# Attention and two gated layers on one core: v's loads moved from SyncE's queue to GpSimd's, q and k requested earlier into more tiles

## The chip, the cores and the metric

The kernel runs on one core of a Trainium2 chip. The time is device microseconds (us) of one execution. A core has TensorE (PE; its weight loads are shown as PEld), VectorE (DVE), ScalarE (ACT), GpSimd (POOL) and SyncE (SP), each with an instruction queue that runs in order, and 16 DMA engines that all queues share.

## The reference

```python
def _attn_ref(q, k, v):                       # each (4, 12, 448, 64)
    S = q.shape[2]
    scale = 1.0 / np.sqrt(q.shape[-1])
    scores = scale * np.matmul(q, k.transpose(0, 1, 3, 2)) - np.log(S)
    attn = 1.0 / (1.0 + np.exp(-scores))
    return np.matmul(attn, v).astype(np.float32)

def reference(**kwargs):
    attn_out = _attn_ref(**attn_kwargs)
    B, H, S, D = attn_out.shape
    x = np.ascontiguousarray(attn_out.transpose(0, 2, 1, 3)).reshape(B * S, H * D)
    x = _moe_ref(x=x, **moe_kwargs)           # x @ w_in, silu, @ w_out: 1792 x 768, 2048 wide
    return _moe2_ref(x=x, **moe2_kwargs)      # x @ w_in, a rational function, @ w_out
```

The two weight pairs of the layers come as float64 arrays, whose bits the kernel turns into float32 itself. The change touches the attention only.

## The kernel before

The program has three stages: attention, the first layer and the second layer. The first 186 us are the attention, and all that follows waits for its output.

Attention works on 24 pairs of heads (NPT). A pair i needs a k tile, a q tile and a v tile, each loaded from DRAM in pieces. `load_by_key` loads k or v of a pair in two DMAs of 128 KB and 96 KB, one for each half of the partitions. q comes in four DMAs of 56 KB, 128 bytes a piece, in a layout that VectorE's 32x32 transpose (`attn_X`) turns into the one that the matmuls need. k is put in order by a copy on GpSimd (`mix`, km from ks), transposed by TensorE (`attn_T`), and split into two parts by ScalarE and VectorE (`attn_C`).

The loop over n has 48 steps, two for each pair, and four for a group of two pairs e and e+1 (`part` is 0 to 3). TensorE's order in a step is: the score matmuls of this step (`attn_QK`, L329), the transposes of a later pair's k (L301, in every second step), and the matmuls with v for the scores of the step before (`attn_AV`, L353). In a group these are 48 score matmuls, eight transposes and 32 matmuls with v. ScalarE applies the sigmoid (L344). `attn_E` copies a finished pair out of PSUM, and for the last two of the four batches stores it in DRAM (L370).

The order on each engine is the order of the code; each queue waits for the tiles that its next instruction needs. In step n = 2i the code calls `mix(i + 2)`, then `load_qk(i + 4)`; the k tile alternates between two buffers, and so does the q tile. In part 0 it also calls `load_v(e + 2)` and `load_v(e + 3)`, into four buffers, after the last matmuls that read the pairs e-2 and e-1. All these loads are issued by SP, but for three of the first pairs' that ACT issues.

SP has other work in this stage. For the layers' weights, `conv_load` (L160) loads 768 KB of a weight into a staging tile, ScalarE and VectorE turn it into float32 (`conv`, called in the steps of `CONVS`), and `conv_out` (L176) stores 384 KB in DRAM. In step 40 (`at_half == -8`) `load_w1` (L526, tile wf) loads the first converted weights of the first layer, which `prep_ij` and `sums_12` (ACT, and DVE L398) read in step 43.

A DMA signals its landing in one of eight counters, which the queues of SP and ACT use in turn. So a load waits until the one eight before it has landed; the program shows this as a wait for DMAHW0 to DMAHW7.

Of the kernel before, what the change touches and what calls it, by code (L numbers as in the profile page):

```python
# [11 lines left out]
F32 = mybir.dt.float32  # L12
# [29 lines left out]
def attention_moe_moe(ctx: ExitStack, tc: tile.TileContext, q, k, v, w_in1, w_out1, w_in2, w_out2, a, b2, out):  # L42
    nc = tc.nc
    B, H, S, D = q.shape
    NT, DM = out.shape
    DFF = w_out1.shape[0]
    P = 128
    NCH = 4
    CP = S // NCH
    NP = H // 2  # L50
    NPT = B * NP
# [14 lines left out]
    def fixed(nm, n, shape, dt, pool=cpool):  # L66
        return [pool.tile(shape, dt, tag=f"{nm}{i}", name=f"{nm}{i}") for i in range(n)]
# [56 lines left out]
    def constants():  # L124
        nc.vector.memset(nls, NEG_LOG_S)
        nc.vector.memset(lnb[:, 0:1], ONE * 2.0**-63)
        nc.vector.memset(lnb[:, 1:2], -63.0 * math.log(2.0))
        nc.scalar.activation(absb[:, 0:1], nls, AF.Sigmoid)
        make_identity(nc, ident)
# [40 lines left out]
    def conv_outs():  # L170
        for do in outs:
            do()
        outs.clear()
# [45 lines left out]
    qs, ks, vs = {}, {}, {}  # L219
    ld_p = [None]  # L220
    ks_t = []
    LO, HI = slice(0, D), slice(D, 2 * D)
    SQ = 32

    def rest_of(i):
        return HI if i % 2 else LO

    def load_by_key(src, t, i, early=False):
        b, hp = divmod(i, NP)
        at_ = 0  # L230
        for part in (LO, HI):
            n = NCH if part == rest_of(i) else NCH - 1
            (nc.scalar if early and part == HI else nc.sync).dma_start(  # L233
                out=t[part, :, : n * D],
                in_=src[b, 2 * hp : 2 * hp + 2, at_ : at_ + n * D].rearrange("h (p c) d -> p h (c d)", c=n),
            )
            at_ += n * D

    def load_qk(i):
        if i >= NPT:  # L240
            return
        b, hp = divmod(i, NP)
        ks[i] = ks_t[i % 2]
        load_by_key(k, ks[i], i, i < 2)
        t = qs[i] = ld_p[0].tile([P, S], F32, tag="qs", name=f"qs_{i}", bufs=2)
        for part in range(2 * D // SQ):
            j, e0 = divmod(part * SQ, D)
            (nc.scalar if i == 0 and part % 2 else nc.sync).dma_start(
                out=t[part * SQ : (part + 1) * SQ, :].rearrange("l (c d) -> l c d", d=SQ),
                in_=q[b, 2 * hp + j, :, e0 : e0 + SQ].rearrange("(c l) d -> l c d", l=SQ),  # L250
            )
# [12 lines left out]
    def load_v(i):  # L264
        if i >= NPT:
            return
        vs[i] = ld_p[0].tile([P, 2, NCH * D], F32, tag="vs", name=f"vs_{i}", bufs=4)
        load_by_key(v, vs[i], i)

    xa_p, xa_s = opened("xa")  # L270
    xa_all = xa_p.tile([P, 9 * 2 * S], F32R, tag="xa_all", name="xa_all")
# [32 lines left out]
    def attn_X(i):  # L304
        x = xq[i] = ld_p[0].tile([P, S], F32, tag="xq", name=f"xq_{i}", bufs=1)
        nc.vector.transpose(x, qs.pop(i))

    def attn_C(i, p, pk, o):
        k_, q_ = st["k", i], st["q", i] = kst.get(), qst.get()
        both = ((k_, o[:, :BK]), (q_, xq.pop(i)))  # L310
        for x, src in both:
            nc.scalar.copy(x[:, 0, :], src)
        for x, src in both:
            nc.vector.tensor_tensor(out=x[:, 1, :], in0=src, in1=x[:, 0, :].bitcast(F32), op=ALU.subtract)
        if p is None:
            pairs.put(pk)
# [45 lines left out]
    def attn_E(i):  # L362
        b, hp = divmod(i, NP)
        del vs[i]
        if b < 2:
            nc.vector.tensor_copy(xk[b * KD + hp], hb[i % 2][:, :S])
            return
        t = xio.get()
        nc.vector.tensor_copy(t[:, :S], hb[i % 2][:, :S])
        nc.sync.dma_start(out=xs[0][hp][:, b * S : (b + 1) * S], in_=t[:, :S])  # L370
        xio.put(t)
# [597 lines left out]
    with tc.manual_schedule():  # L969
# [5 lines left out]
        hb.extend(hb_all[:, j] for j in range(2))  # L975
        hpair.append(hb_all)
        pairs.put(*fixed("pair", 3, [P, 2, 512], F32, ps_p))
        ks_t.extend(fixed("ks", 2, [P, 2, NCH * D], F32, ld_p[0]))
        qst.put(ld_p[0].tile([P, 2, S], F32R, tag="qx", name="qx"))
        load_qk(0)  # L980
        load_qk(1)
        for i in range(2):
            nc.vector.memset(ks_t[i][rest_of(i + 1), :, LAST * D :], 0.0)
        constants()
        warm(11)
# [2 lines left out]
        attn_C(0, *attn_T(0, hb[0]))  # L988
        warm(3)
        mix(1)  # L990
        load_qk(2)
        load_v(0)
        load_v(1)
        load_qk(3)
        conv_load()
        conv_load()

# [4 lines left out]
        for n in range(2 * NPT):  # L1002
            e, part = n // 4 * 2, n % 4
            i, h = divmod(n, 2)
            o = e + 1
            if h == 0:
                mix(i + 2)
                load_qk(i + 4)
            if n < 4:
                units = ([(e, 0), (e, 1)], [(e, 2)], [(o, 0), (o, 1)], [(o, 2), (e, LAST)])[part]  # L1010
                new = (1, 2, NPT, 3)[part]
            else:
                units = ([(e, 0), (e, 1)], [(e, 2), (o, 0)], [(o, 1), (o, 2)], [(e, LAST)])[part]
                new = i + 2 if h else NPT
            conv_outs()
            if new < NPT:
                attn_X(new)
            ready = [(u, attn_QK(*u)) for u in units]
            p = attn_T(new) if new < NPT else None
            for u, p_ in ready:  # L1020
                attn_S(*u, p_)
            for u in waiting:
                attn_AV(*u)
            waiting = units
            if part == 0:
                if e:
                    attn_E(e - 2)
                    attn_E(e - 1)
                load_v(e + 2)
                load_v(e + 3)  # L1030
            if p is not None:
                attn_C(new, *p)
            at_half = n - 2 * NPT
            if at_half >= -NOPS - 6:
                next(first_ops, None)
            flush()
            if at_half == -8:
                load_w1(0)
                load_w1(1)
            if at_half == -5:  # L1040
                xk_s.close()
                wr_p, wr_s = opened("wr")
                wr.extend(fixed("wr", 4, [P, DM], F32R, wr_p))
                wq.extend(fixed("wq", 6, [P, HM], F32R, wr_p))
                prep_ij(0)
                sums_12(0)
            if at_half == -3:
                prep_s12(0)
            if at_half == -1:
                prep_a22(0)  # L1050
            if n == 1:
                stage.put(more)
                conv_load()
                third[0] = more
            if n == 4:
                coefficients()
            if n == 12:
                coefficients_abs()
            if n in CONVS:
                conv()  # L1060
# [247 lines left out]
        for n in range(HN):  # L1308
            g, p = turn(n)
# [25 lines left out]
            if n == 3 * HF - 2:  # L1335
                gsrc.put(wif_all[:, NWS * HM : NWS * HM + BK])
                load_g2(0)
                for i in range(2):
                    t = xa_all[:, 12 * BK + i * DM : 12 * BK + (i + 1) * DM]
                    wring.put(t.rearrange("p (j e) -> p j e", j=2))  # L1340
            if n > 3 * HF:
                i = n - 3 * HF - 1
# [85 lines left out]
```

## Time and profile before

| | |
|---|---|
| median of three runs | 1072.2 us (1068.54 to 1072.66) |
| the profiled execution | 1071.1 us, its span 1069.3 us |
| TensorE busy over the span | 1040.7 us (97%) |
| VectorE, ScalarE, GpSimd busy | 772.8, 604.8, 221.1 us |
| DMA moved | 251.06 MB, mean 235 GB/s |

A busy share is an average over stages. Here the first 186 us differ from the rest: the page's line of TensorE in 40 slices reads 8989987 for them and 9 in all later slices but the last. A matmul that waits for data shows as idle time of TensorE ahead of it, with the instruction or the DMA that came last as its releaser. The issue of a DMA on SP is a row of the queue (SPq); its length is the time until the queue goes on, not the transfer.

### The profile page before, as it was taken

To read this page: it belongs to the slowest core of one execution; us is meant where nothing else is said; L and a number is where in the kernel's file an instruction comes from. 1 tells how busy PE (TensorE), PEld (TensorE's weight loads), DVE (VectorE), ACT (ScalarE), POOL (GpSimd) and SP (SyncE) were. 2 spreads that over 40 slices of the span, in tenths; PEclk is the share of its full clock that TensorE was granted. 3 is DMA by queue.
4 is the path that set the end of the run, shared out by engine and by line. 5 is a ranking of instruction groups with operands and counts; after the bars stand their busy time and mean duration, and the time that the engine had idled before them with its cause. 6 is when DMAs were issued, how large, how long until landed. Compare 5 with 4: busy or idle time off the path is not lost.

```text
span 1069.3 us, 15954 instructions
## 1 busy us (share of the span) xinstructions
PE 1040.7 (97%) x5558; PEld 895.5 (84%) x5558; DVE 772.8 (72%) x1114; ACT 604.8 (57%) x911; POOL 221.1 (21%) x173
## 2 busy tenths in 40 slices
PE   8989987999999999999999999999999999999998
PEld 4545443999998988899998888888999999999998
DVE  4648873788898757877857957779898986545761
ACT  5757874665665544432433448767777866354430
POOL 1110010000000000000000036669877942200000
PEclk9999998999999999999999999999999999999999
DMA  7978775577757676699979953666668979976651
GB/s 171 211 179 217 196 207 177 183 267 268 254 191 258 231 260 215 201 316 351 337 272 336 368 179 100 227 216 216 226 235 295 319 228 307 336 227 198 198 165 52
DMA packets 188896, 251.06 MB, mean 235 GB/s; under 512 B 57360, under 2 KB 142224, under 8 KB 188816
## 3 DMA queue, kind: packets, MB, share of 16 engines
q1 hardware_dynamic: 176736, 230.98, 66.6%
q10 hardware_dynamic: 12016, 19.06, 5.4%
q8 instruction: 43, 0.70, 0.3%
q14 instruction: 37, 0.30, 0.1%
q0 software_dynamic: 64, 0.00, 0.0%
HBM read 166.17 MB, written 83.82 MB: 234 GB/s over the span
## 4 chain that ended last, share of the span: by engine, by line
PE 69%; DVE 12%; DMA 7%; ACT 4%; SPq 3%; issue 3%; POOL 1%; ACTq 0%; DVEq 0%; POOLq 0%
PE hp L925 14%; PE acc L512 13%; PE acc L660 5%; PE acc L661 5%; PE acc L659 5%; PE hb L925 5%; PE hb L512 5%; PE hp L732 3%; PE hp L733 3%; PE hp L734 3%; DMA ks<-in_k_dram 2%; PE hb L353 2%; DVE sb L765 2%; DVE sb L763 2%; SPq L233 2%
## 5 line engine op out<-in xcount | busy, mean ns | idle before, releaser
L381 POOL TENSOR_TENSOR woL<-wif,woH 128x768 fp32r<-128x768 f32 x9 | 17.2, 1930 | 466.6 <-ACT woH L380 466.6
L344 ACT ACTIVATE sb<-pair,nls 128x896 f32<-128x896 f32 x84 | 80.4, 1006 | 30.3 <-PE pair L329 30.0
L659 PE MATMUL acc<-xa_all,woH 128*128 128x512 f32 (+1 forms) x252 | 91.9, 365 | 0.0
L661 PE MATMUL acc<-xa_all,woL 128*128 128x512 f32 (+1 forms) x252 | 91.9, 365 | 0.0
L660 PE MATMUL acc<-xa_all,woH 128*128 128x512 f32 (+1 forms) x252 | 91.9, 365 | 0.0
L353 PE MATMUL hb<-sb,vs 128*64 128x448 f32 (+1 forms) x384 | 77.0, 572 | 7.8 <-DMA vs<-in_v_dram 5.6
L761 POOL TENSOR_TENSOR sb<-sb 128x1024 f32<-128x1024 f32 (+1 forms) x32 | 70.1, 2191 | 39.4 <-ACT sb L758 39.4
L200 ACT ACTIVATE sb<-sb 128x768 f32<-128x768 f32 x64 | 58.0, 906 | 31.6 <-DMA sb<-in_moe_w_in_dram 23.4
L512 PE MATMUL acc<-xb,wr 128*128 128x448 f32 x315 | 68.1, 367 | 0.0
L512 PEld LDWEIGHTS acc<-xb,wr 128*128 128x128 f32 x315 | 59.1, 188 | 5.8 <-issue 0.7
L203 DVE SCALAR_TENSOR_TENSOR sb<-sb 128x768 int32<-128x768 int32 x64 | 61.4, 959 | 2.2
L206 DVE SCALAR_TENSOR_TENSOR sb<-sb 128x768 int32<-128x768 int32 x64 | 61.3, 958 | 2.2
L852 POOL TENSOR_TENSOR sb<-sb 128x384 f32<-128x384 f32 (+1 forms) x43 | 51.1, 1195 | 56.8 <-DMA sb<-gk 54.9
L732 PE MATMUL hp<-hx,woH 128*128 128x512 f32 (+1 forms) x168 | 61.6, 367 | 0.0
L733 PE MATMUL hp<-hx,woH 128*128 128x512 f32 (+1 forms) x168 | 61.6, 367 | 0.0
L734 PE MATMUL hp<-hx,woL 128*128 128x512 f32 (+1 forms) x168 | 61.6, 367 | 0.0
L732 PE MATMUL hp<-xa_all,woH 128*128 128x512 f32 (+1 forms) x168 | 60.7, 362 | 0.0
L734 PE MATMUL hp<-xa_all,woL 128*128 128x512 f32 (+1 forms) x168 | 60.7, 362 | 0.0
L733 PE MATMUL hp<-xa_all,woH 128*128 128x512 f32 (+1 forms) x168 | 60.7, 362 | 0.0
L763 DVE TENSOR_TENSOR sb<-hp,sb 128x768 f32<-128x768 f32 (+1 forms) x31 | 33.6, 1085 | 35.2 <-ACT sb L760 35.2
L329 PEld LDWEIGHTS pair<-xa_all 64*128 64x128 f32 x384 | 34.5, 191 | 26.3 <-issue 12.3
L353 PEld LDWEIGHTS hb<-sb,vs 128*64 128x64 f32 (+1 forms) x384 | 20.7, 138 | 38.0 <-issue 31.7
(241 smaller groups left out, 2738.4 us busy)
## 6 DMA issues: line engine op xcount, KB each, us to landing
sb<-in_moe_w_in_dram SPq DMA_DIRECT2D x32, 768.0 KB, 6.7
sb<-in_moe_w_out_dram SPq DMA_DIRECT2D x32, 768.0 KB, 6.7
gd<-sb SPq DMA_DIRECT2D x64, 224.0 KB, 3.6
wf<-w0i SPq DMA_DIRECT2D x32, 384.0 KB, 3.9
gk<-sb SPq DMA_DIRECT2D x27, 384.0 KB, 4.0
gk<-sb SPq DMA_DIRECT2D x15, 512.0 KB, 3.2
woL<-gk SPq DMA_DIRECT2D x25, 256.0 KB, 4.8
w0i<-sb SPq DMA_DIRECT2D x16, 384.0 KB, 3.2
```

The lines of the kernel that those rows point to most:

```text
L203: nc.vector.scalar_tensor_tensor(out=ui, in0=hi, scalar=SIGN_TOP, in1=ui, op0=ALU.bitwise_and, op1=ALU.bitwise_or)
L344: nc.scalar.activation(t, p[:, :, :S], AF.Sigmoid, bias=nls, scale=QKSCALE)
L353: nc.tensor.matmul(hb[i_ % 2][j * D : (j + 1) * D, :S], vs[i_][part, j, c * D : (c + 1) * D], t[part, j], start=(c == 0), stop=(c == LAST),)
L512: nc.tensor.matmul(o, w_[:, w], x[:, i_, :], start=first and kk == 0 and n_ == 0, stop=kk == HK - 1 and n_ == 2, skip_group_check=not first,)
L659: nc.tensor.matmul(o, woH[c][:, w], x[:, 0, :w_], start=(c == 0), stop=False)
L660: nc.tensor.matmul(o, woH[c][:, w], x[:, 1, :w_], start=False, stop=False)
L661: nc.tensor.matmul(o, woL[c][:, w], x[:, 0, :w_], start=False, stop=(c == KF - 1))
L732: nc.tensor.matmul(o, wh[:, w], x[:, 0, :wd_], start=first, stop=False)
L733: nc.tensor.matmul(o, wh[:, w], x[:, 1, :wd_], start=False, stop=False)
L734: nc.tensor.matmul(o, wl[:, w], x[:, 0, :wd_], start=False, stop=last)
L761: nc.gpsimd.tensor_tensor(out=q_, in0=q_, in1=a_, op=ALU.mult)
L925: nc.tensor.matmul(o, a_, y[:, w_, :], start=kk == 0 and n_ == 0, stop=kk == HF - 1 and n_ == 2)
```

## The change

Five things change. v's loads are issued by GpSimd, not by SP. k has four buffers, not two, and q three, not two (two more memsets on VectorE clear a part of the two new k tiles). The loads of k and q are calls of their own: in an even step 2i the code requests k of the pair i+5, and in the odd step after it q of the pair i+5, where before it requested both of the pair i+4 in the even step. v's loads are called in part 1 of a group instead of part 0. All loads are called after `attn_C` of the step. The order of the computing instructions on TensorE, VectorE, ScalarE and GpSimd stays as it is, but for those two memsets.

```diff
-    def load_by_key(src, t, i, early=False):
+    def load_by_key(src, t, i, eng_hi, eng=nc.sync):
...
-            (nc.scalar if early and part == HI else nc.sync).dma_start(
+            (eng_hi if part == HI else eng).dma_start(
...
-    def load_qk(i):
+    def load_k(i):
+        if i < NPT:
+            ks[i] = ks_t[i % 4]
+            load_by_key(k, ks[i], i, nc.scalar if i < 2 else nc.sync)
+
+    def load_q(i):
         if i >= NPT:
             return
         b, hp = divmod(i, NP)
-        ks[i] = ks_t[i % 2]
-        load_by_key(k, ks[i], i, i < 2)
-        t = qs[i] = ld_p[0].tile([P, S], F32, tag="qs", name=f"qs_{i}", bufs=2)
+        t = qs[i] = ld_p[0].tile([P, S], F32, tag="qs", name=f"qs_{i}", bufs=3)
...
-        load_by_key(v, vs[i], i)
+        load_by_key(v, vs[i], i, nc.gpsimd, nc.gpsimd)
...
-        ks_t.extend(fixed("ks", 2, [P, 2, NCH * D], F32, ld_p[0]))
+        ks_t.extend(fixed("ks", 4, [P, 2, NCH * D], F32, ld_p[0]))
...
-        load_qk(2)
         load_v(0)
         load_v(1)
-        load_qk(3)
+        load_k(2)
+        load_q(2)
+        load_k(3)
+        load_q(3)
+        load_k(4)
         conv_load()
         conv_load()
...
             if h == 0:
                 mix(i + 2)
-                load_qk(i + 4)
...
+            if p is not None:
+                attn_C(new, *p)
+            if h == 0:
+                load_k(i + 5)
+            if n == 0 or h:
+                load_q(i + (5 if h else 4))
+            if part == 1:
                 load_v(e + 2)
                 load_v(e + 3)
-            if p is not None:
-                attn_C(new, *p)
```

On SP, this is a piece of the queue before, from steps 6 to 10. In brackets stands what a row waits for: DMAHW is the landing of an earlier load, DVE, PE and Pool are the last readers of the buffer. ks, qs and vs are the tiles of k, q and v.

```order
L233 DMA ks_247<-in_k_dram 64x2x256 [waits DMAHW1_49,Pool_49]
L233 DMA ks_247<-in_k_dram 64x2x192 [waits DMAHW2_49]
L248 DMA qs_455<-in_q_dram 32x14x32 [waits DMAHW3_49,DVE_49]
L248 DMA qs_455<-in_q_dram 32x14x32 [waits DMAHW4_49]
L248 DMA qs_455<-in_q_dram 32x14x32 [waits DMAHW5_49]
L248 DMA qs_455<-in_q_dram 32x14x32 [waits DMAHW6_49]
L233 DMA vs_482<-in_v_dram 64x2x256 [waits DMAHW7_49,PE_49]
L233 DMA vs_482<-in_v_dram 64x2x192 [waits DMAHW0_49]
L233 DMA vs_485<-in_v_dram 64x2x192 [waits DMAHW1_49,PE_49]
L233 DMA vs_485<-in_v_dram 64x2x256 [waits DMAHW2_49]
L233 DMA ks_248<-in_k_dram 64x2x192 [waits DMAHW3_49,Pool_49]
L233 DMA ks_248<-in_k_dram 64x2x256 [waits DMAHW4_49]
```

The four loads of v stand between the loads of two pairs, and k of the later pair is behind v's wait for TensorE. This is SP's queue after the change in the same place.

```order
L233 DMA ks_250<-in_k_dram 64x2x192 [waits DMAHW7_49,Pool_49]
L233 DMA ks_250<-in_k_dram 64x2x256 [waits DMAHW0_49]
L251 DMA qs_518<-in_q_dram 32x14x32 [waits DMAHW1_49,DVE_49]
L251 DMA qs_518<-in_q_dram 32x14x32 [waits DMAHW2_49]
L251 DMA qs_518<-in_q_dram 32x14x32 [waits DMAHW3_49]
L251 DMA qs_518<-in_q_dram 32x14x32 [waits DMAHW4_49]
L176 DMA w0i_105<-sb 128x768 [waits DMAHW5_49,DVE_49]
L160 DMA sb<-in_moe_w_in_dram 128x6x256 [waits DMAHW6_49,Activation_49]
L233 DMA ks_247<-in_k_dram 64x2x256 [waits DMAHW7_49,Pool_49]
L233 DMA ks_247<-in_k_dram 64x2x192 [waits DMAHW0_49]
```

No row of v is left in it, and no row waits for TensorE; w0i is the store of a converted weight, which now carries a wait for VectorE's work as well. On GpSimd this is the queue before around step 4, where the two small loads of the second layer's coefficients (ab) stand.

```order
L260 COPY km_385<-ks_248 128x2x4x64 [waits DMAHW6_49,DMAHW7_49,PE_49,Pool_49]
L260 COPY km_451<-ks_247 128x2x4x64 [waits DMAHW6_49,DMAHW7_49,PE_49,Pool_49]
L133 DMA ab<-in_moe_a_dram 128x4
L134 DMA ab<-in_moe_b_dram 128x2
L260 COPY km_523<-ks_248 128x2x4x64 [waits DMAHW1_49,DMAHW2_49,PE_49,Pool_49]
L260 COPY km_579<-ks_247 128x2x4x64 [waits DMAHW1_49,DMAHW2_49,PE_49,Pool_49]
```

It holds copies, each of which waits for k's two loads. This is GpSimd's queue after the change.

```order
L263 COPY km_462<-ks_247 128x2x4x64 [waits DMAHW0_49,DMAHW1_49,PE_49,Pool_49]
L133 DMA ab<-in_moe_a_dram 128x4 [waits DMASW0_49]
L134 DMA ab<-in_moe_b_dram 128x2 [waits DMASW1_49]
L233 DMA vs_523<-in_v_dram 64x2x256 [waits DMASW2_49,PE_49]
L233 DMA vs_523<-in_v_dram 64x2x192 [waits DMASW3_49]
L233 DMA vs_526<-in_v_dram 64x2x192 [waits DMASW4_49,PE_49]
L233 DMA vs_526<-in_v_dram 64x2x256 [waits DMASW5_49]
L263 COPY km_534<-ks_248 128x2x4x64 [waits DMAHW5_49,DMAHW4_49,Pool_49]
L263 COPY km_590<-ks_249 128x2x4x64 [waits DMAHW0_49,DMAHW7_49,PE_49,Pool_49]
```

Every second copy now has v's four loads ahead of it, with their wait for TensorE; GpSimd's loads signal in eight counters of their own (DMASW).

## Rows read from the trace of the kernel before

**Rows 1.** By stretch: us; PE, PEld, DVE, ACT, POOL busy; clock, DMA share, GB/s

```profile
0.00:186.00 186.00, 165.12 (x1071) 85.96 (x1072) 115.91 (x187) 125.31 (x171) 18.95 (x31) 0.97 0.78 195
186.00:1069.00 883.00, 875.58 (x4488) 809.52 (x4487) 656.91 (x928) 479.44 (x740) 202.16 (x142) 1.00 0.71 243
```

**Rows 2.** What TensorE waited for, 20 to 186 us: total, times, longest

```profile
PE pair L301 <- POOL km L260: 5.8, 5, 2.3
PE hb L353 <- DMA vs<-in_v_dram: 5.3, 2, 4.4
PE pair L329 <- ACT sb L344: 3.7, 2, 2.0
```

**Rows 3.** TensorE's timeline: start, length, instructions, idle time before and its releaser

```profile
52.94 0.98 PE L353 MATMUL hb<-sb,vs 64*64 64x448 f32 x8
...
73.64 3.25 PE L353 MATMUL hb<-sb,vs 128*64 128x448 f32 x8 [4.41 <-DMA vs<-in_v_dram]
...
87.95 1.72 PE L353 MATMUL hb<-sb,vs 128*64 128x448 f32 x8
...
100.66 1.72 PE L353 MATMUL hb<-sb,vs 128*64 128x448 f32 x8
...
113.59 1.72 PE L353 MATMUL hb<-sb,vs 128*64 128x448 f32 x8
...
127.27 1.72 PE L353 MATMUL hb<-sb,vs 128*64 128x448 f32 x8
...
141.86 1.72 PE L353 MATMUL hb<-sb,vs 128*64 128x448 f32 x8
...
171.78 0.88 PE L329 MATMUL pair<-qx,xa_all 64*128 64x448 f32 x6 [2.01 <-ACT sb L344]
174.92 3.25 PE L353 MATMUL hb<-sb,vs 128*64 128x448 f32 x8 [2.25 <-DVE sb L369]
```

**Rows 4.** Granted clock where TensorE resumes after the two long waits, columns as above

```profile
72.00:76.00 4.00, 2.36 (x8) 0.85 (x8) 0.00 (x0) 0.00 (x0) 0.61 (x1) 0.70 0.43 75
...
176.00:180.00 4.00, 4.00 (x18) 1.79 (x14) 0.60 (x1) 0.32 (x1) 0.00 (x0) 0.57 0.56 206
```

**Rows 5.** SP's timeline: start, length from first to last issue, loads

```profile
65.14 2.67 SPq L233 DMA_DIRECT2D vs<-in_v_dram  x4
...
127.33 1.32 SPq L233 DMA_DIRECT2D ks<-in_k_dram  x2
...
137.71 2.60 SPq L233 DMA_DIRECT2D vs<-in_v_dram  x4
140.36 0.59 SPq L176 DMA_DIRECT2D w0i<-sb  x1
141.05 0.39 SPq L160 DMA_DIRECT2D sb<-in_moe_w_in_dram  x1
141.54 0.66 SPq L233 DMA_DIRECT2D ks<-in_k_dram  x1
```

**Rows 6.** The chain that ended last, 140 to 187 us: start, length, what

```profile
166.71 0.58 SPq L526
...
167.34 5.29 DMA wf<-w0i
...
172.65 0.57 DVE sf L398
```

**Rows 7.** GpSimd's two loads and its copies of k: length in ns, min/median/max

```profile
L133 POOL DMA_DIRECT2D ab<-in_moe_a_dram x1: 707/707/707, 26.1 to 26.1; - x1
...
DMA to landing us min/median/max: 3.4/3.4/3.4
L260 POOL COPY km<-ks x23: 610/614/1382, 6.9 to 163.7; 128x512 f32<-128x512 f32 x23
```

**Rows 8.** Loads, 0 to 186 us: how many, KB each, median us to landing

```profile
sb<-in_moe_w_in_dram SPq DMA_DIRECT2D x14, 768.0 KB, 7.0
...
ks<-in_k_dram SPq DMA_DIRECT2D x23, 128.0 KB, 5.5
```

More of the change, by code (lines that the diff above doesn't have):

```diff
@@ L977, in attention_moe_moe @@
         pairs.put(*fixed("pair", 3, [P, 2, 512], F32, ps_p))
-        ks_t.extend(fixed("ks", 2, [P, 2, NCH * D], F32, ld_p[0]))
+        ks_t.extend(fixed("ks", 4, [P, 2, NCH * D], F32, ld_p[0]))
         qst.put(ld_p[0].tile([P, 2, S], F32R, tag="qx", name="qx"))
-        load_qk(0)
-        load_qk(1)
         for i in range(2):
+            load_k(i)
+            load_q(i)
+        for i in range(4):
             nc.vector.memset(ks_t[i][rest_of(i + 1), :, LAST * D :], 0.0)
```

## The prediction

> **What bounds the kernel now.** I read the busy time by stretch first [rows 1]. From 186 us on TensorE is busy in 875.6 of 883 us, so only work taken off TensorE would help there, and the change takes none. In the first 186 us TensorE is busy 165.1 us, and no other engine is nearer to full: VectorE 115.9, ScalarE 125.3, GpSimd 19.0. All that follows waits for the attention, so what the change can give is TensorE's idle time in this stretch, about 21 us, and what its clock loses behind it.
>
> Next I read whom TensorE waited for once the first pairs are through [rows 2]. GpSimd's copies of k held up five transposes, 5.8 us in total. Two loads of v held up the matmuls with v, 5.3 us. The row for ScalarE holds one wait of 2.0 us from the last steps, which I come to below.
>
> Then the timeline shows why the loads were late. TensorE's matmuls from 52.94 us are the last readers of the v tiles that the loads of step 12 fill [rows 3]; from then on these loads could have gone out. SP issued them at 65.14 us [rows 5], and TensorE stood 4.41 us before it could go on at 73.64 us [rows 3]. SP was 11 us behind the program. It doesn't catch up: from the k load at 127.33 us to its counterpart one group (four steps) later at 141.54 us it needs 14.21 us [rows 5], and TensorE's group beside it, from 127.27 to 141.86 us, takes 14.59 us [rows 3]. SP's rows follow one another without a wait there (v ends at 140.31 us, the store begins at 140.36), so it is not SP that waits for the program. Where no load is late, a group takes TensorE 12.71 us (87.95 to 100.66) and 12.93 us (100.66 to 113.59) [rows 3]. So in the later half of the stage SP's queue sets the pace, and a load that comes late is late because its turn in that queue was late.
>
> The end of the stage has the same cause. The first layer's weights are requested in step 40 and read in step 43, but SP issues them only at 166.71 us; they land 5.29 us after the last but two was issued, and VectorE starts on them at 172.65 us [rows 6]. ScalarE and VectorE run in order, so the sigmoid and the copy out of PSUM stand behind them, and TensorE waits 2.01 and 2.25 us [rows 3].
>
> **The change part by part.** *v off SP.* Four loads of v are 2.60 to 2.67 us of SP in each group [rows 5]. Without them the group at 127.33 us costs SP 14.21 - 2.60 = 11.6 us, less than TensorE's 12.7 to 12.9 us. SP then waits for the program, not the program for SP. It is a small margin, 1.1 us in a group; behind every load of 768 KB, which takes a median of 7.0 us to land [rows 8], the queue still stretches, since each load waits for the one eight before it.
>
> *More tiles, earlier requests.* k of the pair i+5 is requested in step 2i and copied by GpSimd in step 2i+6; before it had four steps. q gets six steps, and its wait for VectorE's transpose (the tile's last reader) is now for work of the same step, no longer of the next one, so less stands still behind it on SP: k, the stores and the weights. Six steps are one and a half groups, 19 us, against a landing of 5.5 us for k [rows 8]. That covers the waits that are left on SP. If SP still fell behind by 1 us a group, ten groups would eat 10 of these 19 us, so the k waits would still go.
>
> *v on GpSimd.* 48 loads are added there. The nearest rows are its two loads of 128 small pieces, the longer issue 0.707 us, the landing 3.4 us; a v load has 128 pieces too, but of 768 or 1024 bytes [rows 7]. At 0.71 us four loads and two copies of 0.61 us are 4.1 us a group, of 12.7. The worst end: GpSimd's copy takes 0.61 us as a rule but 1.38 us once [rows 7]; with every load and copy stretched by that factor of 2.3, it is 6.4 + 2.8 = 9.2 us, and still fits. I take 0.71 us, the row nearest in kind and number of pieces. Queued behind v's loads is the copy of k for the odd pair, which has two steps until its transpose; ahead of them is the wait for TensorE to be done with the pairs e-2 and e-1, in part 0. The loads go out then, five steps or 16 us before they are needed in part 1 of the next group; four issues of 0.71 us and a landing of 3.4 us leave 9 to 10 us of slack. What GpSimd's writes may cost VectorE no row shows; a gain there is excluded, since nothing leaves either engine. The lower bound is 0 (22 of 23 copies need not have met anybody, the median 614 ns is the minimum within 4 ns), the upper bound 48 times the copy's 0.77 us, 37 us, if each one delayed VectorE and TensorE waited for each. I take 0.5 us, near the lower end, as the copies' median is there.
>
> The Trainium skill has a rule that speaks against this part ("SBUF — State Buffer", under "A bandwidth-pool intuition that's wrong", the box on the "DVE blocks DMA" trap): GpSimd builds the descriptors of its loads in software, and cannot write them while VectorE holds the port that both share. The same section gives a load of about 620 ns that took about 3100 ns beside a VectorE copy; by an estimate from that figure four loads and two copies would be 13.6 us a group, more than TensorE needs. No run here shows it yet; it is the third rival below, with a price from rows.
>
> *Two memsets.* They run while VectorE waits for the first k, and cost nothing; if not, a few tenths of a us at the start.
>
> **The sum.** Waits for v 5.3 and for k 5.8 [rows 2]; the weights at the end 2.01 + 2.25 = 4.3 [rows 3]. Behind both long waits TensorE starts at the lower of its two levels, 1.2 GHz: the granted clock is 0.70 from 72 to 76 us and 0.57 from 176 to 180 us [rows 4], after an idle time of 4.41 us in one case and of 2.01 and 2.25 us in the other, and the eight matmuls after each take 3.25 instead of 1.72 us [rows 3]. That is 2 x 1.53 = 3.1 us more. Together 18.5 us. Back from it I take 2.0 us, as groups that no load holds up still differ by 0.22 us (12.71 and 12.93) and nine groups are concerned, and the 0.5 us for VectorE: 16.0 us. What is late next is TensorE itself: ScalarE and VectorE have 125.3 and 115.9 us of work [rows 1] for the 169 us that the stage would take, and they kept up in the groups of 12.71 and 12.93 us. After 186 us all is only earlier. The profiled execution took 1071.1 us, 1.1 below the median of the runs; 1071.1 - 16.0 = 1055 us.
>
> **The rivals.** *The DMA engines are the bound.* They are busy at a share of 0.78 over the 186 us [rows 1], 145 us of work which the change keeps whole. If early requests collide and the share cannot rise above 0.83, the stage needs 145 / 0.83 = 175 us, a gain of 11 and a time of 1060 us. With more collisions it is less. For it: loads of 5.5 and 7.0 us to land [rows 8]. Against it: the v loads at 65.14 us were late by their turn on SP, not by their transfer.
>
> The Trainium skill says the same from the other side ("DMA: Bandwidth & Descriptors", under "Issuing engines are not separate DMA queues"): loads from any queue run on the same 16 engines, and another queue saves only the time to issue. By that the gain is SP's 2.6 us a group, and it exists only where SP was the bound; the trace agrees in so far as SP had no wait from 137.71 to 141.54 us [rows 5].
>
> *SP stays behind.* If the landing of one load in eight, and not the number of loads, sets SP's pace, the loads of 768 KB hold it as before, and groups stay at 14 us. Then the k waits and the weights at the end stay; v's 5.3 us may go and some turn up elsewhere. That is 1071 less 0 to 5, about 1069 us. The change would then not do what it says: requests would be written earlier and not be issued earlier. Against it: the four loads of v take their 2.60 us of SP in a piece without a wait.
>
> *GpSimd becomes the bound: slower.* If a load of v holds GpSimd until it has landed, at the 3.4 us of the small load [rows 7], a group costs it 4 x 3.4 + 1.2 = 14.8 us, 2.1 more than TensorE's 12.7, in eleven groups 23 us; set against the forecast that is 1078 us. It decides from (12.7 - 1.2) / 4 = 2.9 us a load. Against it: the issue of 0.71 us.
>
> **How the numbers follow.** Forecast, 1050 to 1060 us: 0.65. DMA engines, 1060 to 1066: 0.17. SP behind, about 1069: 0.10. GpSimd the bound, about 1078: 0.08. A difference of 0.5%, 5.4 us, is about what a measurement of this kernel can tell from no change. So faster 0.82, same 0.10, slower 0.08. The range reaches from 1049 (all of the 18.5 us, the 1.7 us that ScalarE's row [rows 2] holds beside its 2.0, and some of the runs' spread) to 1066 (the DMA rival), which leaves out the two others: 0.8.
>
> **What would show it.** Right: no wait of TensorE for v or for GpSimd's copies over 1 us after the first steps; groups of 12.7 to 13.2 us; the weights of step 40 landed before step 43, no idle time of 2 us in the last steps and no lower clock there; SP idle between loads, waiting for VectorE; the first layer starts at about 170 us instead of 186. Wrong: v loads of over 2.9 us each on GpSimd, or copies of k that wait behind them; SP's queue without gaps and groups of 14 us; a DMA share of over 0.85 with loads that take 8 us and more to land.

## The result and the profile after

The changed kernel takes 1054.85 us (median of four runs, 1054.72 to 1056.27), the kernel before beside it 1072.13 us. The ratio is 0.9849 with an interval of 0.9826 to 0.9872: 1.5% faster. The profiled execution took 1054.81 us, its span 1053.0 us. Lines of the code behind the loads are three higher than before (the sigmoid's L344 is now L347).

The first view is the busy time by stretch, with the columns of [rows 1]. The stage is the attention; a group is four steps, two pairs of heads.

```profile
0.00:170.00 170.00, 159.09 (x1060) 84.34 (x1062) 120.26 (x188) 124.33 (x170) 45.11 (x79) 1.00 0.90 214
170.00:1053.00 883.00, 877.16 (x4502) 810.25 (x4498) 655.50 (x928) 480.07 (x742) 201.19 (x142) 1.00 0.71 243
```

TensorE's 165 us of work in the attention now take some 14 us less. The granted clock is 1.00 over the stage, where it was 0.97 [rows 1]. VectorE is busy 120.26 us, 4.4 more than before, although two memsets are all that it got. That is the first sign of the step that failed.

The next view is what TensorE waited for, 20 to 170 us (total, times, longest).

```profile
PE pair L332 <- DVE xa_all L317: 5.1, 5, 1.5
PE hb L356 <- DVE xk L369: 1.3, 2, 0.8
PE pair L332 <- ACT sb L347: 1.3, 1, 1.3
```

The waits for v and for k of [rows 2] are gone. A new one has come: five waits for the last instruction of `attn_C` on VectorE (L317), which needs q's transpose. The timeline of TensorE shows them (columns of [rows 3]):

```profile
118.88 0.98 PE L356 MATMUL hb<-sb,vs 64*64 64x448 f32 x8
...
127.84 0.88 PE L332 MATMUL pair<-xa_all 64*128 64x448 f32 x6 [0.98 <-DVE xa_all L317]
...
132.96 0.98 PE L356 MATMUL hb<-sb,vs 64*64 64x448 f32 x8
...
141.85 1.50 PE L332 MATMUL pair<-xa_all 64*128 64x448 f32 x12 [1.18 <-DVE xa_all L317]
...
146.97 0.98 PE L356 MATMUL hb<-sb,vs 64*64 64x448 f32 x8
...
171.68 3.57 PE L515 MATMUL acc<-xb,wr 128*128 128x448 f32 x16
```

The small matmuls with v (64*64) come once in a group, so their starts give the groups: 14.08 and 14.01 us here, where no load is late. The last row is the first layer. It starts at 171.68 us; before, it started at 185.76 us.

GpSimd's rows are the two below: v's loads (length of one issue in ns, min/median/max), and its copies of k.

```profile
L233 POOL DMA_DIRECT2D vs<-in_v_dram x48: 587/594/756, 7.4 to 150.0; - x48
...
L263 POOL COPY km<-ks x23: 610/629/1252, 6.9 to 150.6; 128x512 f32<-128x512 f32 x23
```

A v load costs GpSimd 0.594 us. SP's own longest wait and its timeline show that SP no longer sets the pace:

```profile
SPq L176 <- DVE sb L206: 15.8, 6, 3.4
```

```profile
122.67 1.55 SPq L233 DMA_DIRECT2D ks<-in_k_dram  x2
126.69 0.32 SPq L176 DMA_DIRECT2D w0i<-sb  x1
...
149.63 1.98 SPq L529 DMA_DIRECT2D wf<-w0i  x4
```

Behind the k load at 122.67 us SP stands until VectorE has converted the weight that it is to store (L176). The first layer's weights go out from 149.63 us, seventeen us earlier than in [rows 6].

Now the new wait. These are VectorE's timeline and, beside it, GpSimd's.

```profile
122.51 1.56 DVE L201 TENSOR_SCALAR sb<-sb 128x768 f32<-128x768 f32 x1 [0.20 <-ACT sb L200]
124.11 0.56 DVE L202 TENSOR_SCALAR sb<-sb 128x768 int32<-128x768 int32 x1
124.71 0.96 DVE L203 SCALAR_TENSOR_TENSOR sb<-sb 128x768 int32<-128x768 int32 x1
125.70 0.96 DVE L206 SCALAR_TENSOR_TENSOR sb<-sb 128x768 int32<-128x768 int32 x1
126.58 0.64 DVE L309 STREAM_TRANSPOSE xq<-qs 128x448 f32<-128x448 f32 x1
...
127.84 0.63 DVE L317 TENSOR_TENSOR xa_all<-xq,xa_all 128x448 fp32r<-128x448 f32 x1
```

```profile
120.16 2.33 POOL L233 DMA_DIRECT2D vs<-in_v_dram  x4 [11.12 <-PE hb L356]
122.48 1.18 POOL L263 COPY km<-ks 128x512 f32<-128x512 f32 x2
```

The weight conversion (L201 to L206) stands ahead of q's transpose (L309) in VectorE's order; TensorE resumes at 127.84 us, when L317 begins to deliver. L201 takes 1.56 us while GpSimd copies k from 122.48 to 123.66 us; 0.56 us is its usual time. The loads of v, from 120.16 us, stretch nothing. I took for each VectorE instruction of the stage its time above the shortest of its own form. Beside copies of k this comes to 5.8 us in 22 instructions (before: 1.9 us in 28); beside issues of v alone, to 0.26 us in 38.

The Trainium skill describes such a thing ("SBUF — State Buffer", under "SBUF: two separate sides"): VectorE, in certain modes or with two inputs from SBUF, and GpSimd use one pair of ports, and the one that holds it blocks the other for the whole instruction. The rows agree in size: 1.56 is 0.56 and about one us of the 1.18 us of copies; in which mode L201 runs no row shows. The Trainium skill's "DVE blocks DMA" trap, a box in the same section, which the prediction weighed, isn't seen in the issues: the slowest of 48 took 756 ns.

### The profile page after: what moved, and what is told of

It is laid out like the page before. It is cut to its first block, busy times and chain, and to the rows that moved or that the text cites. A ratio compares the mean times of both kernels' runs of the same rounds, so it can differ in the third digit from the quotient of the medians.

```text
span 1053.0 us, 15972 instructions
## 1 busy us (share of the span) xinstructions
PE 1036.2 (98%) x5558; PEld 894.6 (85%) x5558; DVE 775.8 (74%) x1116; ACT 604.4 (57%) x911; POOL 246.3 (23%) x221
## 4 chain that ended last, share of the span: by engine, by line
PE 72%; DVE 11%; ACT 5%; DMA 4%; issue 3%; POOL 3%; SPq 2%; ACTq 0%; DVEq 0%; POOLq 0%
PE acc L515 14%; PE hp L928 13%; PE acc L663 5%; PE acc L664 5%; PE acc L662 5%; PE hb L515 5%; PE hb L928 5%; PE pair L332 3%; PE hp L735 3%; PE hp L737 3%; PE hp L736 3%; PE hb L356 3%; POOL sb L855 2%; PE hb L663 2%; PE hb L664 2%
## 5 line engine op out<-in xcount | busy, mean ns | idle before, releaser
L347 ACT ACTIVATE sb<-pair,nls 128x896 f32<-128x896 f32 x84 | 80.7, 1010 | 17.0 <-PE pair L332 16.7
L356 PE MATMUL hb<-sb,vs 128*64 128x448 f32 (+1 forms) x384 | 73.9, 554 | 1.3 <-DVE xk L369 1.3
L206 DVE SCALAR_TENSOR_TENSOR sb<-sb 128x768 int32<-128x768 int32 x64 | 61.3, 958 | 2.2
L332 PE MATMUL pair<-xa_all 64*128 64x448 f32 x384 | 50.8, 391 | 3.5 <-DVE xa_all L317 2.7
```

Of the source, the lines that this page charges most:

```text
L332: nc.tensor.matmul(p[:, j, :S], K[rows[j], a_, c * P : (c + 1) * P], Q[rows[j], b_, :], start=(n == 0), stop=(n == len(turns) - 1),)
L347: nc.scalar.activation(t, p[:, :, :S], AF.Sigmoid, bias=nls, scale=QKSCALE)
L356: nc.tensor.matmul(hb[i_ % 2][j * D : (j + 1) * D, :S], vs[i_][part, j, c * D : (c + 1) * D], t[part, j], start=(c == 0), stop=(c == LAST),)
```

## The experiments

Each run's ratio is to the kernel before on the same chip, whose median was 1069.8 to 1072.1 us there. The starts of the first layer are read from TensorE's timeline.

| kernel | median us | ratio, interval | first layer starts |
|---|---|---|---|
| changed kernel | 1054.85 | 0.9849, 0.9826 to 0.9872 | 171.68 |
| changed, v back on SP | 1076.81 | 1.0034, 1.0013 to 1.0055 | 193.31 |
| before, v alone on GpSimd | 1051.62 | 0.9795, 0.9776 to 0.9814 | 166.85 |
| the same, and SP given other loads | 1072.42 | 1.0028, 1.0009 to 1.0047 | 186.76 |
| before, first weights requested earlier | 1072.3 | 1.0003, 0.998 to 1.0025 | 190.54 |
| changed, conversions a step later | 1050.5 | 0.9784, 0.9766 to 0.9801 | 167.70 |
| changed, conversions moved to part 2 | 1054.82 | 0.9841, 0.9807 to 0.9875 | 170.23 |
| v alone on GpSimd, conversions a step later | 1051.62 | 0.9817, 0.9776 to 0.9857 | 167.02 |
| v alone, and k's tiles and lead | 1057.45 | 0.9878, 0.9845 to 0.9911 | 174.1 |
| v alone, and q's tiles and place | 1056.66 | 0.9863, 0.9831 to 0.9895 | 171.1 |
| changed, v's place as before | 1055.69 | 0.9855, 0.9825 to 0.9885 | 172.9 |

Two more kernels ran once and have no interval: GpSimd filled with memsets (1139.13 us), and v's bytes moved twice (1058.62 us).

**Which part gives the gain.** First the change with v's loads back on SP, tiles and lead kept:

```diff
-        load_by_key(v, vs[i], i, nc.gpsimd, nc.gpsimd)
+        load_by_key(v, vs[i], i, nc.sync, nc.sync)
```

> The changed kernel with v's loads back in SP's queue (called in part 1 as now); four k tiles, three q tiles and the early requests stay. Theory (SP's queue was the pace, v's four loads of 2.6 us a group are what made it so): SP needs about 14 us a group again, falls behind TensorE by over 1 us a group and uses up the six steps of lead; v comes late again, since its lead is bound by its four tiles: about 1063 us, with waits of TensorE for v. Rival (the longer lead alone cures it, GpSimd's queue is not needed): 1055 us and no such waits.

Measured: 1076.81 us, slower than before, and 14 us above what I expected. TensorE's longest list of waits, and SP's timeline:

```profile
PE hb L356 <- DMA vs<-in_v_dram: 15.2, 7, 5.2
```

```profile
129.09 4.05 SPq L251 DMA_DIRECT2D qs<-in_q_dram  x4
133.24 4.72 SPq L233 DMA_DIRECT2D vs<-in_v_dram  x4
...
145.37 4.98 SPq L251 DMA_DIRECT2D qs<-in_q_dram  x4
```

SP needs 16.3 us for a group, and its rows follow one another. Two rows are longer than their issues: the first, of q, behind a load of 768 KB, and v's, 4.72 us where 2.60 is usual [rows 5]. Tiles and lead make no room on a full queue; they put k and q ahead of v, and v is late instead. Then v's move alone, in the kernel before:

```diff
-    def load_by_key(src, t, i, early=False):
+    def load_by_key(src, t, i, early=False, eng=nc.sync):
...
-        load_by_key(v, vs[i], i)
+        load_by_key(v, vs[i], i, eng=nc.gpsimd)
```

> The kernel before with v's loads issued by GpSimd in part 0, and nothing else: two k tiles, two q tiles, old requests. Theory (SP's queue was the pace): SP has 11.6 us of work a group and catches up; waits for v gone, waits for k mostly gone, the weights of step 40 issued in time: 1056 to 1060 us. Rival (the tiles and the lead matter as much, since q's request still waits for a transpose of the next step): waits for k stay at 3 us or more, 1062 to 1066 us.

Measured: 1051.62 us, below the range that I expected and 3 us less than with the whole change (6 us by the ratios, as the two were timed on different chips); the two ratios' intervals don't meet. The views are TensorE's waits and GpSimd's timeline.

```profile
PE pair L329 <- ACT sb L344: 1.5, 1, 1.5
PE hb L353 <- DVE xk L366: 1.3, 2, 0.8
PE pair L329 <- DVE xa_all L314: 0.8, 1, 0.8
```

```profile
118.24 2.34 POOL L233 DMA_DIRECT2D vs<-in_v_dram  x4 [5.83 <-PE hb L353]
124.48 0.62 POOL L260 COPY km<-ks 128x512 f32<-128x512 f32 x1 [3.90 <-DMA ks<-in_k_dram]
```

No wait for k is left although k keeps its two tiles and its old lead. k lands later here, so the copy follows v's loads by 3.9 us and comes alone; by then the conversion is over.

**Is it the number of issues on SP?** The same kernel, with SP given as many loads in v's places, of 8 KB from DRAM to DRAM, which nothing reads and which wait for nobody on TensorE:

```diff
+        for part in range(2):
+            few = dr_p.tile([P, 2, 16], F32, tag=f"few{i}_{part}", name=f"few{i}_{part}")
+            nc.sync.dma_start(out=few[:D], in_=v[b, 2 * hp : 2 * hp + 2, part * D : (part + 1) * D, :16].rearrange("h p d -> p h d"))
```

> The kernel before with v's loads on GpSimd, and in their places on SP as many loads of 8 KB (128 pieces of 64 bytes, DRAM to DRAM, nobody reads them, no wait for TensorE). So SP has its old number of issues, nearly without v's bytes and without v's wait. Theory (the number of issues, 0.6 us each in a queue that runs in order and lets eight be in flight, is what made SP the pace): most of the gain is lost, 1064 to 1072 us, with waits for k. Rival (it was v's bytes in SP's ring, or the wait for TensorE ahead of them): 1052 to 1056 us.

Measured: 1072.42 us. All of the gain is gone, and the wait is for k again:

```profile
PE pair L305 <- POOL km L260: 13.1, 8, 4.5
```

```profile
124.13 2.78 SPq L272 DMA_DIRECT2D few<-in_v_dram  x4
126.97 0.58 SPq L176 DMA_DIRECT2D w0i<-sb  x1
...
132.89 3.85 SPq L233 DMA_DIRECT2D ks<-in_k_dram  x2
...
139.98 2.52 SPq L272 DMA_DIRECT2D few<-in_v_dram  x4
```

Four tiny loads take 2.5 to 2.8 us of SP, as v's did [rows 5], and the group from 124.13 us is 15.85 us. So neither v's bytes nor its wait for TensorE made SP late; the number of loads in its queue decides. But the issues alone do not fill the period. Before, this row stands in the group of 14.21 us from 127.33 us:

```profile
128.74 3.83 SPq L248 DMA_DIRECT2D qs<-in_q_dram  x4
```

Four loads of q take 2.10 us elsewhere in that group, two of k 1.32 [rows 5]; here, behind a load of 768 KB, q's take 3.83 and the next two of k 1.75 us. Without these 2.2 us the group is 12.0 us, less than TensorE's 12.7. In the run with the tiny loads q's row behind that load is 3.27 us and k's 3.85; without the 3.7 us that they are longer the group is 12.1 us. So SP is late by the issues and the time that it stands behind the large load together. Only the first was changed here; whether smaller loads of the weights would free SP as well was not tried.

**Can the end be mended alone?** In the kernel before the first layer's weights are requested in step 36, not 40:

```diff
-            if at_half == -8:
+            if at_half == -12:
```

> The kernel before with the first layer's weights requested in step 36 instead of 40, and nothing else. By the sum's term for the end of the stage (waits of 2.01 and 2.25 us, the lower clock behind them 1.5 to 2.1 us) they land before step 43: 1072 - 6 = 1066 us. Rival: the four loads of 384 KB only move the lateness to k and v of the last pairs: 1070 to 1072 us.

Measured: 1072.3 us, no change. In the waits of TensorE the weights no longer appear; k does:

```profile
PE pair L301 <- POOL km L260: 11.0, 4, 6.7
PE hb L353 <- DMA vs<-in_v_dram: 3.3, 1, 3.3
```

On this queue, which is late, a request moved ahead makes another one late.

**The DMA engines.** Each v load of the changed kernel is issued a second time, from DRAM to DRAM, 5.5 MB more:

```diff
+        vx = dr_p.tile([P, 2, NCH * D], F32, tag=f"vx{i}", name=f"vx{i}")
+        load_by_key(v, vx, i, nc.gpsimd, nc.gpsimd)
```

> The changed kernel with every v load issued a second time by GpSimd, from DRAM to a DRAM buffer that nobody reads: 5.5 MB more in the attention, on 36 MB. Theory (the queue was the bound, not the 16 DMA engines): 1055 to 1058 us. Rival (the engines are nearly full, a share of 0.9 in this stage): their work grows by some 15%, and the stage by 10 to 20 us, 1065 to 1075 us.

Measured: 1058.62 us, in one run. The stage by its busy times:

```profile
0.00:168.00 168.00, 154.47 (x1028) 81.55 (x1030) 122.04 (x188) 121.80 (x167) 74.39 (x127) 1.00 0.96 249
```

The engines' share rises to 0.96 and the rate to 249 GB/s, at a price of some 4 us, and TensorE still waits for no load (its longest waits are 5.4 us for L319, which is L317 of the changed kernel, and 2.7 us for ScalarE). VectorE's stretch beside copies is 8.4 us here, so the price need not be that of the engines. At 0.90 they were not the bound. The share is no measure of how full they are: in the changed kernel it reads 1.06 from 60 to 80 us.

**GpSimd as the bound.** Eight memsets of the v tile, thrown-away work, go ahead of each pair's two loads:

```diff
+        for _ in range(8):
+            nc.gpsimd.memset(vs[i], 0.0)
```

> The changed kernel with eight memsets of the v tile (128x512) on GpSimd ahead of each pair's two loads: work that is thrown away, to lengthen GpSimd's part of a load. Theory (GpSimd has room up to 2.9 us a load, 11.5 us a group): if the memsets are 0.3 us each, a load costs 0.6 + 1.2 = 1.8 us and a group 8.4 us, so the time stays within 1 to 3 us of the changed kernel's 1055, the rest being the port; at 0.6 us each it is 3.0 us a load, at the limit, and over 1058. Rival (v's loads are already near late, their issue on GpSimd is on the path): every microsecond on GpSimd shows, 16 memsets a group x 0.3 us x 11 groups = 53 us and more.

Measured: 1139.13 us, in one run. GpSimd's timeline, and TensorE's wait over the whole span:

```profile
60.81 5.20 POOL L272 MEMSET vs<- 128x512 f32 x8 [6.08 <-PE hb L358]
...
73.56 1.18 POOL L263 COPY km<-ks 128x512 f32<-128x512 f32 x2
81.00 4.64 POOL L272 MEMSET vs<- 128x512 f32 x8 [6.26 <-PE hb L358]
```

```profile
PE pair L306 <- POOL km L263: 64.4, 12, 8.7
```

A group is 20.2 us, though GpSimd works only 13.9 of them: it waits 6.3 us for TensorE, then TensorE waits for the copies behind the memsets. The two take turns. This bound is real, and it is a round trip and not a sum of GpSimd's work.

**Is the new wait the conversion ahead of q's transpose?** In the changed kernel the conversions from step 18 on, but that of step 21, come a step later, all but the first of them at the end of part 1, behind q's transpose of that step and after the two copies of k:

```diff
-        CONVS = (2, 5, 8, 11, 15, 18, 21, 24, 28, 32, 36, 40)
+        CONVS = (2, 5, 8, 11, 15, 19, 21, 25, 29, 33, 37, 41)
```

> The changed kernel with six of the twelve weight conversions moved by one step, from steps 18, 24, 28, 32, 36, 40 to 19, 25, 29, 33, 37, 41. After an even step the next one begins with q's transpose on VectorE, which then stands behind 3 us of conversion; after an odd step none follows. Theory (what TensorE still waits for, 5.1 us in five waits on the scores' right side, is q's transpose behind the conversion): the five waits go, 1049 to 1051 us. Rival (VectorE and ScalarE are full, the wait turns up elsewhere): 1054 to 1056 us.

Measured: 1050.5 us. TensorE's waits:

```profile
PE pair L332 <- ACT sb L347: 2.3, 1, 2.3
PE hb L356 <- DVE xk L369: 1.9, 3, 0.8
```

The wait for L317 is gone, and VectorE's stretch beside copies falls from 5.8 to 1.5 us. This edit takes away both the transpose behind the conversion and the meeting with the copies. To part them, the conversions went to part 2:

```diff
+        CONVS = (2, 5, 8, 11, 15, 18, 22, 26, 30, 34, 38, 42)
```

> The changed kernel with six weight conversions moved from steps 21, 24, 28, 32, 36, 40 to 22, 26, 30, 34, 38, 42. They still stand just ahead of q's transpose on VectorE, but no longer start in part 0, where GpSimd comes free of its wait for TensorE and copies k of two pairs in a row. Theory (the port that VectorE shares with GpSimd's copies of k is what stretches the conversion; the stretch is 5.8 us in the changed kernel, 1.9 before): the stretch falls to about 2 us and the time to about 1051.5 us, near the kernel that has only v moved. Rival (it is the place of the transpose behind 3 us of conversion, stretched or not): four or five waits of about 1 us stay, 1053.5 to 1055.5 us.

Measured: 1054.82 us, the time of the changed kernel. The stretch beside copies is down to 2.4 us, and TensorE's waits are others:

```profile
PE pair L332 <- ACT sb L347: 2.8, 6, 1.0
...
PE pair L332 <- DVE xa_all L317: 0.4, 1, 0.4
```

Less contention alone brought nothing. VectorE's and ScalarE's timelines show why:

```profile
117.82 0.64 DVE L309 STREAM_TRANSPOSE xq<-qs 128x448 f32<-128x448 f32 x1
...
118.49 0.56 ACT L315 CAST qx<-xq 128x448 fp32r<-128x448 f32 x1 [2.77 <-DVE xq L309]
```

q's transpose still stands behind the conversion, which takes its usual time there (L201 0.55 us, at 114.77). ScalarE waits 2.77 us for the transpose, and its sigmoids, for which TensorE waits, come behind that. The group from 117.72 us is 14.10 us; all of the 1.4 us above 12.7 lie ahead of 122.03 us, in the waits of 0.39 us for L317, 0.52 us for ScalarE and idle times too short for the list. So the place of the conversion costs as much here as the stretch does in the changed kernel, as the rival of this run had it. With v alone on GpSimd, the conversion moved as in the run of 1050.5 us:

> The kernel before with v's loads on GpSimd and the conversions of steps 18, 24, 28, 32, 36, 40 one step later; two k tiles and two q tiles as before. Theory (what is left in the kernel with only v moved are waits of 3.6 us in all, of which 0.8 stand behind a conversion): 1050 to 1051.5 us, about the same as the changed kernel with the moved conversions (1050.5). Rival (each brings its own gain, 21 us from v and 4 from the conversions): 1047 to 1048 us.

Measured: 1051.62 us. It adds nothing to the time, since with v alone the wait for L314 was only 0.8 us. The profiled execution shows two differences that cancel. From 37.81 us on its groups take 1.6 us less than those of v alone; from the last small matmul to the first layer it takes 12.8 us (154.24 to 167.02) instead of 11.0 (155.84 to 166.85), as ScalarE waits 2.4 us for the first layer's weights. The two edits mostly mend the same thing.

**Which of the other parts costs these 3 to 6 us?** k's part, q's part, and the place of v's calls were tried apart. k's, on top of v alone on GpSimd (the main lines):

```diff
+            if h == 0:
+                load_k(i + 5)
...
-        ks_t.extend(fixed("ks", 2, [P, 2, NCH * D], F32, ld_p[0]))
+        ks_t.extend(fixed("ks", 4, [P, 2, NCH * D], F32, ld_p[0]))
```

> The version with v's loads on GpSimd alone (1051.6 us), plus k's part of the change: four k tiles and k requested five pairs ahead at the end of the step; q and the place of v's loads stay as they were. It asks which part costs the 3 us between 1051.6 and 1054.9. Theory: k. With k landed early GpSimd's copy runs as soon as its own tile is free, which is beside VectorE's conversions, and stretches them: 1054 to 1055.5 us, TensorE waits of 3 us or more in sum for VectorE's last part of q and k (the line of xa_all), and VectorE's work beside copies stretched by 4 us or more in the stage, as in the changed kernel (5.8). Rival: q or v's place does it: 1051 to 1052 us, waits for xa_all of under 1.5 us, a stretch of 2 to 3.5 us.

Measured: 1057.45 us (1055.90 to 1062.71), more than expected. The profiled execution took 1059.88 us; its waits are

```profile
PE pair L332 <- ACT sb L347: 3.5, 2, 2.2
PE pair L332 <- DVE xa_all L317: 3.2, 5, 1.0
```

with a stretch of VectorE beside copies of 4.9 us. Its first layer starts 7.3 us later than with v alone, and 4.2 of these lie behind the last small matmul (158.88 to 174.12, 15.2 us instead of 11.0): the first layer's weights go out at 155.51 us, where it was 148.39, ScalarE waits 1.8 us for them, TensorE 2.2 us for ScalarE, and from 164 to 168 us the granted clock is 0.68. That is a loss at the end of the stage and not the stretch. The quickest of its runs, with a clock of 1.000, still took 1055.9 us. q's, on top of the same:

```diff
+            if n == 0 or h:
+                load_q(i + (5 if h else 4))
```

> The version with v's loads on GpSimd alone (1051.6 us), plus q's part of the change: three q tiles and q requested behind the step's own work; k and the place of v's loads stay as they were. Theory (k costs the 3 us): 1051 to 1052 us, since SP has time to spare and q has no copy on GpSimd. Rival (q costs them, as the requests of one eighth of the loads behind the stores delay the stores and the 768 KB loads): 1054 to 1055.5 us.

Measured: 1056.66 us. TensorE waits 2.6 us for L317 and 2.7 us for the copies of k; the stretch is 4.0 us. The place of v's calls, in the changed kernel:

```diff
             if part == 0:
                 if e:
                     attn_E(e - 2)
                     attn_E(e - 1)
+                load_v(e + 2)
+                load_v(e + 3)
...
-            if part == 1:
-                load_v(e + 2)
-                load_v(e + 3)
```

> The changed kernel (1054.9 us) with v's loads put back from the end of part 1 of a group to part 0, where the kernel before has them; k's and q's tiles and lead as changed. Theory (k costs the 3 us): 1054 to 1055.5 us, waits for xa_all of 3 us or more. Rival (v's place costs them, since in part 1 its four issues push the copy of k for the odd pair onto VectorE's work): 1051 to 1052 us, waits for xa_all of under 1.5 us.

Measured: 1055.69 us, waits for L317 of 5.0 us in 5: no difference from the changed kernel, though the stretch is 7.1 us. GpSimd waits for the same matmuls of TensorE in either place.

So the theory that k alone costs them fell. Each of the two is enough, and they don't add up. The sums of the stretch do not rank the kernels (v alone has 3.2 us), since some of it falls where nobody waits for VectorE. One group shows what it costs where TensorE waits, the one that holds the L201 of the changed kernel above. The rows are those of v alone, of k's part, of q's part, and of v's calls put back:

```profile
120.60 0.56 DVE L201 TENSOR_SCALAR sb<-sb 128x768 f32<-128x768 f32 x1 [0.19 <-ACT sb L200]
```

```profile
121.67 1.03 DVE L201 TENSOR_SCALAR sb<-sb 128x768 f32<-128x768 f32 x1 [0.20 <-ACT sb L200]
```

```profile
122.98 1.03 DVE L201 TENSOR_SCALAR sb<-sb 128x768 f32<-128x768 f32 x1 [0.19 <-ACT sb L200]
```

```profile
123.73 1.59 DVE L201 TENSOR_SCALAR sb<-sb 128x768 f32<-128x768 f32 x1 [0.20 <-ACT sb L200]
```

| kernel | L201, us | its group, us | group less L201 |
|---|---|---|---|
| v alone on GpSimd | 0.56 | 13.09 | 12.53 |
| v alone, and k's tiles and lead | 1.03 | 13.54 | 12.51 |
| v alone, and q's tiles and place | 1.03 | 13.54 | 12.51 |
| changed kernel | 1.56 | 14.08 | 12.52 |
| changed, v's place as before | 1.59 | 14.09 | 12.50 |

With the conversion ahead of q's transpose, the group grows by what the copies add to L201. The last five groups of the changed kernel are 4.0 us longer than those of v alone, of the 4.8 us by which its first layer starts later.

For k the trace shows how the two meet: k has landed when v's loads go out, so the copy follows at once and meets the conversion. q has no work on GpSimd. That its place in SP's order moves k's landing (the copy at 122.95 us runs beside L201, in the kernel with v alone at 124.48 us it does not) is read from one trace and wasn't tried by itself.

## Why the prediction was right, and where it was not

The time was right: 1055 us forecast, 1054.85 measured. Not all of the steps were.

- **The bound**: right in the main. SP's queue made the loads late. Taking four issues a group off SP gives the whole gain, and giving as many back takes it all. But one reading was wrong. The loads of v at 65.14 us were called "late by their turn on SP, not by their transfer". The chain that ended last, in the kernel before, has this row there:

```profile
65.87 7.63 DMA vs<-in_v_dram
```

These loads were issued just behind one of 768 KB and took 6.9 to 8.1 us to land; the median of v's loads was 2.7 us. TensorE went idle at 69.23 us, so with that median they would have come in time even at their late turn. So the wait of 4.41 us needed both, the late turn and the slow landing. With v on GpSimd no wait for v is left; the two were not parted.

- **v off SP** and **the end of the stage**: right. No wait for v or k is left, the weights go out at 149.63 us, SP waits for VectorE, and the granted clock is 1.00. The four terms of the sum, 18.5 us, are gone; the 1.3 us that TensorE still waits for ScalarE stand at 22.93 us, at the start of the stage, and had 1.65 us before.
- **More tiles, earlier requests**: this step failed. It was to cover "the waits that are left on SP". None were left: v alone on GpSimd takes 1051.6 us. Without v's move the step makes the kernel slightly slower than before (1.0034), and on top of it it costs 3 to 6 us.
- **v on GpSimd**: the issue was 0.594 us, against 0.71 taken, and v was never late. The landing is 4.3 us against 3.4. The term of 0.5 us for VectorE was too small. VectorE is stretched by 3.9 us more than before, and TensorE waits 5.1 us for it. It was also looked for at the wrong place. The copy's median in [rows 7] was near its minimum, and I took that for a sign that they seldom meet. But VectorE is stretched too, so its rows were to be read. And not v's loads meet VectorE, but the copies of k that now come right behind them.
- **What is late next**: "ScalarE and VectorE kept up" failed. They kept up in the two groups of 12.7 and 12.9 us quoted. In the later groups the conversion stands ahead of q's transpose. The groups below are from one small matmul with v to the next.

| kernel | the last six groups of the stage, us |
|---|---|
| before | 12.70, 12.72, 13.55, 14.94, 15.06, 13.97 |
| changed | 12.70, 13.37, 14.62, 14.08, 14.01, 13.69 |
| v alone on GpSimd | 12.69, 12.95, 13.90, 13.09, 12.90, 12.89 |
| changed, conversions a step later | 13.32, 12.72, 12.70, 12.69, 12.72, 12.70 |

I had forecast 12.7 to 13.2 us. In the later half one bound gave place to another: the conversion ahead of q's transpose, stretched by the copies.

- **The sum**: the stage gained 14.1 us (185.76 to 171.68), not 16.0. The time came out right since the stages behind took 881.3 us, 2.2 less than before's 883.5. In the runs with an interval that part was 881.0 to 884.7 us, with no order that I could find, so I put it down to no cause. The two differences cancelled, and that is luck: the sum held back 2.5 us, where the new wait alone took 5.1.
- **The rivals**: the DMA engines were not the bound; the share of 0.83 that this rival took for a ceiling was passed at 0.90, and again at 0.96. "SP stays behind" fell with SP's waits for VectorE, but what it named is part of the bound: 2.2 us of SP's 14.21 us passed behind the load of 768 KB. GpSimd was far from its limit, but the rival's price was wrong. With memsets a load cost 3.06 us of GpSimd (two in 6.12 us); by the rival's sum a group is then 13.4 us, and it was 20.2.

## What to carry to other kernels

Before adding tiles or lead, add up what the late queue issues in a period, and what it stands behind its large loads, and compare that with the period of the engine that computes. Here, where that sum was larger, moving loads to an idle queue helped and requesting earlier did not. Once a load is no longer late, look at what now runs at the same time as what, and read the stretch in the rows of each engine that may lose, not of the one that is moved. Where two small edits mend the same wait (here, v alone on GpSimd at 1051.6 us, or the whole change with the conversions a step later at 1050.5 us), the plainer one is enough.

## What the runs showed of the hardware

- A VectorE instruction beside GpSimd's copies of 128x512 float32 took 1.56 instead of 0.56 us; beside GpSimd's issue of loads it took its usual time (38 instructions, 0.26 us in all).
- Loads of v issued by GpSimd land after a median of 4.3 us, where the median of the same loads from SP was 2.7 us; here that cost nothing.
- Loads of v issued on SP right behind a load of 768 KB landed after 6.9 to 8.1 us (the four from 65.14 us of the kernel before).
- With a DMA share of 0.96 over 168 us, at 249 GB/s, TensorE waited for no load in the stage.
